# Weight splits, residual loads and table loads re-placed around the sixteen steps of an FFT convolution, with three store buffers

## The chip, the cores and the metric

The kernel runs on one core of a Trainium2 chip. The metric is device time in microseconds (us) of one execution. The kernel before was run three times: 688.23, 689.53 and 689.91 us, median 689.53.

A core has a matrix engine (TensorE, in the profile PE, its weight loads PEld), three engines for elementwise work (VectorE, DVE; ScalarE, ACT; GpSimd, POOL) and a sync engine (SyncE, SP), which here does nothing but issue transfers. An engine runs its own instructions in order. A transfer (DMA) is issued by an engine, onto that engine's queue, and carried out by the core's 16 DMA engines, which all queues share.

## The reference

One block with conditioned layer norms. A long convolution comes first (part A), a gated mixing network behind it (part B). Cut to what matters, with `L = 2048`, `D = 512` and `F = 1376`:

```python
h = layernorm(x) * (1 + ca) + sa                  # x is u; sa..gb = silu(c) @ w_mod
# part A: state-space convolution along L
K = einsum("dn,dnl,dn->dl", C, exp(dt * A * l), dt * B).real
y = irfft(rfft(pad(h)) * rfft(pad(K)))[:, :L] + h * Dskip
x = x + ga * y
h = layernorm(x) * (1 + cb) + sb
# part B: token mixing by shifts, then channel mixing
g = gelu(layernorm(h) @ w1)
x1 = h + concat(g[+1], g[-1], g[+2], g[-2]) @ w2   # each quarter of g shifted along L
x = x + gb * (x1 + gelu(layernorm(x1) @ w3) @ w4)
```

## The kernel before

**Stages.** From 0 to about 207 us the kernel generates the convolution kernel K, normalises the input, transforms it and stores that spectrum to a scratch tensor `VU` in DRAM. Then comes the second half of the convolution, which is the place of the change, up to about 316 us. The rest, to the end, is part B: products with `w1`, `w2`, `w3`, `w4`, bound by PE.

**The convolution as small transforms.** A transform of length 4096 is cut into small matrix products with tables of cosines and sines. `k_first` (line 619) is the first transform of K, eight rounds of 16 matmuls with the table `FK`; ACT and DVE copy the results out of PSUM into `VK`. Then follow sixteen *steps* `(jh, kc)`, for two halves of the channels (`jh`) and eight groups of four frequencies (`kc`). A step n consists of

- `spectrum_k` (line 664): the second transform of K, 32 matmuls with the table `T2` into two PSUM tiles `pk`. A part of them needs the negative of a piece of `T2`; that negative is a tile `T3`, which `flip` (line 658) makes on POOL, two instructions for two steps.
- `multiply` (line 685): on DVE, four products of `pk` with the input's spectrum `us` (line 690, tiles `ma` and `mb`) and two sums (line 692, tiles `zc`).
- `back` (line 695): eight short matmuls with the table `Gm` into `pz`, for the step before (n - 1); ACT copies them to a tile `z`, and POOL issues two transfers that store `z` to the scratch tensor `ZT[jh]` in DRAM (line 706). `z` comes from the pool `s2` with two buffers, so that ACT may write a new `z` only when the store of the one before the last has landed.
- `spectrum_u` (line 642) for step n + 1: PE reads a block `ld` of `VU`, and ACT copies the results to `us`.

DVE, ACT and POOL run this in the order in which it is written here (`manual_schedule`).

**The transfers.** Blocks `ld` (0.524 MB each) come from a pool `ldp` with seven buffers. A block holds a part of `VU` for `spectrum_u` (`load_vu`, line 640, issued three steps ahead), or a part of `ZT` for the inverse transform (`load_inv`, line 721), or two quarters of `w1`. SP issues all of these, the four pieces of the residual x (`load_x`, 1.05 MB each, into the tile `X2`, which the profile calls `KX` after the buffer it reuses), the table `FI` of the inverse transform (1.05 MB, during step 9) and `w2`.

**The inverse** of a half `jh` needs all eight `kc` of `ZT[jh]`. It is cut into four groups g of two halves each (`inv_half`, line 726): 16 half-size matmuls from four blocks, and DVE adds the result to `X2` (line 734). `inverse(0, 0)` stands in step 12, `inverse(0, 3)` in step 13, `inverse_parts(0, 1)` in step 15. For `ZT(0)` the four blocks of the first groups are asked for in step 10, and the other four in step 13.

**Behind the steps.** The last store of `ZT(1)` is issued by SP and ACT in two parts, and its reads follow at once (lines 1167 ff.). Until they land, PE has little to do: `inv_half(0, 2, ...)` from `ZT(0)`, and `keep(6)` (line 1180, its matmuls line 1165), six matmuls on a quarter of `w1h` whose result nobody uses. In the profile the first inverse matmuls from `ZT(1)` write the PSUM tile `py`. The text calls this stretch the hole.

**Split weights.** Each weight matrix is used as a sum of two parts. ACT makes the high part, `w1h` or `w2h` (line 115, the helper `act`), and DVE the rest, `w1l` or `w2l`, by a subtraction (line 756). `w1` and `w2` have four such pairs each. The splits of `w1` stand in steps 9 and 10 and work from blocks `ld`; those of `w2` stand in steps 14 and 15 and work in place, out of `w2l`. `w2`, `w3` and `w4` were copied earlier from the inputs to scratch tensors `Dw` in DRAM by POOL's queue, beside the generation of K; `w1` is read from the input.

Of the kernel before, what the change touches and what calls it, by code (L numbers as in the profile page):

```python
# [106 lines left out]
def body(ctx, tc, A):  # L107
# [12 lines left out]
    WD = {k: dpool.tile(list(A[k].shape), F32, name="D" + k) for k in ("w2", "w3", "w4")}  # L120
# [390 lines left out]
    for k in range(2):  # L511
        side[28 + 3 * k].append(lambda i=k * 256: P.dma_start(WD["w2"][i:i + 256], A["w2"][i:i + 256]))
# [94 lines left out]
    Gm = c2.tile([128, 2, 64], F32, name="Gm")  # L607
# [3 lines left out]
    ldp = a2.enter_context(pool("ldp", bufs=7))  # L611
# [44 lines left out]
    t3s = {}  # L656

    def flip(kc):
        t = t3s[kc] = c2.tile([128, 8, 64], F32, name="T3", bufs=3)
        for gh in range(2):  # L660
            r = slice(gh * 64, gh * 64 + 64)
            P.tensor_scalar(t[r], T2[kc // 4][r, kc % 4 * 4:kc % 4 * 4 + 8, 64 - gh * 64:128 - gh * 64], -1.0, None, op0=OP.mult)

    def spectrum_k(jh, kc):
        p = [kbank([128, 2, 2, 128]) for gh in range(2)]
        for i in range(2):
            for ro in range(2):
                for ri in range(2):
                    for kk in range(2):
                        for gh in range(2):  # L670
                            k1 = kc * 4 + 2 * kk + i
                            rows = slice(gh * 64, gh * 64 + 64)
                            w = T2[k1 // 16][rows, k1 % 16]
                            if ri == gh:
                                w = w[:, ro * 64:ro * 64 + 64]
                            elif ro == ri:
                                w = w[:, gh * 64:gh * 64 + 64]
                            else:
                                w = t3s[kc // 2 * 2][rows, k1 % 8]
                            T.matmul(p[gh][kk * 64:kk * 64 + 64, i, ro], w,  # L680
                                     VK[jh][rows, ri * 32 + k1].rearrange("p j g -> p (j g)"),
                                     start=(ri == 0), stop=(ri == 1), skip_group_check=True)
# [12 lines left out]
    def back(jh, kc):  # L695
        zc = zcs.pop((jh, kc))
        z = s2.tile([128, 4, 256], F32, name="z")
# [25 lines left out]
    def load_x(g):  # L723
        Y.dma_start(X2[:, g * 4:g * 4 + 4].rearrange("p b d -> p (b d)"), A["x"][g])
# [18 lines left out]
    def weights(pl, src, rows, cols, name, ntile):  # L743
# [3 lines left out]
        def load(stage, i, m=1, c0=0, c1=cols):  # L747
            n = min(128, rows - i * 128)
            w = stage(m, c1 - c0) if stage else lo.bitcast(F32)[:, i:i + m, c0:c1]
            Y.dma_start(w[:n], src[i * 128:i * 128 + (m - 1) * 128 + n, c0:c1].rearrange("(a p) n -> p a n", p=n))  # L750
# [8 lines left out]

    def two(m, n):  # L760
        return block().rearrange("p (a c) b -> p a (c b)", a=2)
# [335 lines left out]
    with tc.manual_schedule():  # L1097
        load_vu(*steps[0])
        flip(0)
        Y.dma_start(Gm, A["G"].rearrange("p (a b) -> p a b", a=2))  # L1100
        for r in range(8):
            k_first(r)
            if r == 3:
                load_vu(*steps[1])
            if r == 6:
                load_vu(*steps[2])
        us = spectrum_u(*steps[0])
        split = None
        for n, st in enumerate(steps):
            p = spectrum_k(*st)  # L1110
            multiply(*st, us, p)
            if n == 7:
# [4 lines left out]
                W1h, W1l, ldw1 = weights(pw1, A["w1"], 512, 512, "w1", 4)  # L1117
# [6 lines left out]
            if n + 3 < 16:  # L1124
                load_vu(*steps[n + 3])
            if n % 2 == 0 and n < 14:
                flip(steps[n + 2][1])
            if n in (3, 4, 6, 8):
                load_x(n - 3 if n < 5 else n // 2 - 1)
            if n == 9:  # L1130
                Y.dma_start(FI, A["FI"].rearrange("p (a b c) -> p a b c", a=32, b=2))
            if split:
                split()
                split = None
            if n in (8, 9):
                split = ldw1(two, n % 2 * 2, 2)
# [12 lines left out]
            if n in (14, 15):  # L1149
                w2s.pop()()  # L1150
# [24 lines left out]
        for b in (14, 15, 4, 5, 6, 7):  # L1175
            half_stat(b, 0)
        for k in (1, 2):
# [124 lines left out]
```

## Time and profile before

| | |
|---|---|
| median of three runs | 689.53 us |
| the profiled execution, its own time | 691.26 us |
| its span | 689.5 us |
| PE busy (weight loads) | 642.6 us (509.2) |
| DVE busy | 498.0 us |
| ACT busy | 331.2 us |
| POOL busy | 124.8 us |
| moved by DMA | 86.42 MB, 125 GB/s on average |

The span runs from the first instruction to the last; the execution's own time holds a little more at its ends. Busy PE over the whole kernel says that part B and the generation of K are PE's. The page's 40 slices show where this is not so (each digit is a tenth of the slice, a slice is 17.2 us, and the 14th to the 19th hold 224 to 327 us):

```profile
PE   1899999999999998977998999999999999999996
DVE  7899999999996887986987967464574536363522
ACT  3878988889875557432444623123131312222121
POOL 4011112112103355413741101001010000000000
DMA  8603264643739997967387010020100201010001
GB/s 299 284 2 79 75 218 105 209 121 85 275 85 317 354 335 258 346 204 226 108 257 240 1 32 32 16 77 15 47 31 17 77 1 62 1 49 13 1 31 31
```

From the 13th to the 19th the row DMA stands between 6 and 9, and the row GB/s between 204 and 354; behind the 22nd both are low. How to read a row of the chain of waits, in what follows: the time at which a piece of work in the chain began, its length, the engine or DMA, and the tile. A row of the waits names who waited and for whom: total us, count, the longest.

### The profile page before, as it was taken

The numbers are of one execution on the slowest core, as the hardware profiler recorded it, in microseconds if no ns is written. First come the engines' busy times: TensorE is split into PE (matmuls) and PEld (weight loads), VectorE is DVE, ScalarE is ACT, GpSimd is POOL, SyncE is SP. The second block draws the span as 40 slices with busy tenths as digits, with TensorE's granted clock in tenths as the row PEclk, the third lists the DMA queues.
The fourth block names the chain that finished last, engine by engine and source line by source line (L and its number), as shares of the span: only waits on it lengthen the run. The fifth ranks groups of instructions, "written<-read, shape, count | busy, mean of one in ns | idle before, by whom it ended". The sixth has DMA issues, their size and how long they took to land.

```text
span 689.5 us, 16884 instructions
## 1 busy us (share of the span) xinstructions
PE 642.6 (93%) x7195; PEld 509.2 (74%) x7195; DVE 498.0 (72%) x795; ACT 331.2 (48%) x505; POOL 124.8 (18%) x236
## 2 busy tenths in 40 slices
PE   1899999999999998977998999999999999999996
PEld 0456655655569776634887889999899889898895
DVE  7899999999996887986987967464574536363522
ACT  3878988889875557432444623123131312222121
POOL 4011112112103355413741101001010000000000
PEclk9999999999999999998999999999999999999999
DMA  8603264643739997967387010020100201010001
GB/s 299 284 2 79 75 218 105 209 121 85 275 85 317 354 335 258 346 204 226 108 257 240 1 32 32 16 77 15 47 31 17 77 1 62 1 49 13 1 31 31
DMA packets 51091, 86.42 MB, mean 125 GB/s; under 512 B 4676, under 2 KB 39496, under 8 KB 48424
## 3 DMA queue, kind: packets, MB, share of 16 engines
q1 hardware_dynamic: 46712, 66.74, 30.1%
q0 software_dynamic: 3440, 17.57, 7.4%
q8 instruction: 56, 0.92, 0.6%
q10 hardware_dynamic: 864, 1.05, 0.5%
q14 instruction: 19, 0.16, 0.1%
HBM read 59.12 MB, written 32.90 MB: 133 GB/s over the span
## 4 chain that ended last, share of the span: by engine, by line
PE 70%; DVE 6%; DMA 5%; ACT 3%; POOL 2%; issue 1%; ACTq 0%; SPq 0%; DVEq 0%; POOLq 0%
PE pm L841 7%; PE pm L838 7%; PE pm L839 7%; PE xx L448 7%; PE pa L954 6%; PE pa L955 6%; PE pa L962 6%; PE kp L498 3%; DMA ZT<-z 3%; PE ph L893 2%; PE ph L895 2%; PE ph L892 2%; DMA ld<-ZT 2%; PE pu L426 2%; PE pT L803 2%; PE pk L626 2%
## 5 line engine op out<-in xcount | busy, mean ns | idle before, releaser
L115 ACT ACTIVATE gh<-pm 128x512 fp32r<-128x512 f32 (+1 forms) x48 | 26.9, 560 | 200.7 <-PE pm L841 200.7
L838 PE MATMUL pm<-nh,w3h 128*128 128x256 f32 (+1 forms) x352 | 86.6, 281 | 2.7 <-ACT nh L115 2.7
L839 PE MATMUL pm<-nh,w3l 128*128 128x256 f32 (+1 forms) x352 | 86.3, 280 | 0.1
L946 DVE TENSOR_TENSOR gl<-gf,gh 128x512 fp32r<-128x512 f32 (+1 forms) x48 | 30.8, 643 | 68.4 <-ACT gf L115 68.4
L954 PE MATMUL pa<-w4h,gh 128*128 128x512 f32 (+1 forms) x176 | 69.6, 395 | 0.0
L838 PEld LDWEIGHTS pm<-nh,w3h 128*128 128x128 f32 (+1 forms) x352 | 66.0, 187 | 4.4 <-ACT nh L115 2.9
L955 PE MATMUL pa<-w4l,gh 128*128 128x512 f32 (+1 forms) x176 | 68.9, 392 | 0.0
L839 PEld LDWEIGHTS pm<-nh,w3l 128*128 128x128 f32 (+1 forms) x352 | 65.9, 187 | 2.2 <-DVE w3l L756 0.5
L765 POOL TENSOR_TENSOR rs<-mv,eps_t 128x1 f32<-128x1 f32 (+1 forms) x39 | 11.0, 282 | 282.4 <-DVE mv L771 265.4
L841 PE MATMUL pm<-nl,w3h 128*128 128x256 f32 (+1 forms) x352 | 55.0, 278 | 0.0
L449 PE MATMUL xx<-MG,ON 64*128 64x512 f32 x160 | 48.1, 397 | 0.0
L962 PE MATMUL pa<-w4h,gl 128*128 128x512 f32 (+1 forms) x176 | 48.0, 390 | 0.0
L448 PE MATMUL xx<-MG,ON 64*128 64x512 f32 x160 | 48.0, 396 | 0.0
L841 PEld LDWEIGHTS pm<-nl,w3h 128*128 128x128 f32 (+1 forms) x352 | 47.0, 187 | 0.0
L898 DVE TENSOR_TENSOR h<-h,ph 128x512 f32<-128x512 f32 x16 | 11.0, 687 | 45.1 <-PE ph L895 45.1
L466 DVE SCALAR_TENSOR_TENSOR e<-tr,p 128x512 f32<-128x512 f32 x64 | 41.1, 684 | 1.5 <-ACT tr L115 1.5
L498 PEld LDWEIGHTS kp<-e,e 128*32 128x32 f32 x2048 | 30.1, 110 | 12.7 <-issue 7.6
L475 DVE TENSOR_TENSOR e<-tr,p 128x1024 f32<-128x1024 f32 x32 | 39.0, 1220 | 0.0
L476 DVE TENSOR_TENSOR e<-tr,m 128x1024 f32<-128x1024 f32 x32 | 39.0, 1219 | 0.0
L115 ACT ACTIVATE p<-xx 128x1024 f32<-128x1024 f32 (+1 forms) x40 | 37.5, 979 | 2.2 <-PE xx L252 1.0
L962 PEld LDWEIGHTS pa<-w4h,gl 128*128 128x128 f32 (+1 forms) x176 | 33.0, 188 | 7.3 <-DVE gl L946 0.2
L115 ACT ACTIVATE tr<-xx 128x1024 f32<-128x1024 f32 x32 | 33.0, 1030 | 9.6 <-PE xx L449 7.9
(236 smaller groups left out, 1731.6 us busy)
## 6 DMA issues: line engine op xcount, KB each, us to landing
VU<-vs SPq DMA_DIRECT2D x64, 128.0 KB, 3.7
ld<-VU SPq DMA_DIRECT2D x16, 512.0 KB, 7.4
ZT<-z POOLq DMA_DIRECT2D x30, 256.0 KB, 6.2
ld<-ZT SPq DMA_DIRECT2D x12, 512.0 KB
Dw<-in_w POOLq DMA_DIRECT2D x8, 688.0 KB, 4.7
xu<-in_u SPq DMA_DIRECT2D x4, 1024.0 KB, 8.0
KX<-in_x SPq DMA_DIRECT2D x4, 1024.0 KB, 8.0
GD<-go SPq DMA_DIRECT2D x16, 256.0 KB, 2.3
```

The costliest lines, as they stand in the source:

```text
L115: return S.activation(out, in_, f, bias=bias, scale=scale)
L448: T.matmul(x[:, :512], la, ma, start=(i == 0), stop=(i == len(ops) - 1))
L449: T.matmul(x[:, 512:], lb, mb, start=(i == 0), stop=(i == len(ops) - 1))
L466: V.scalar_tensor_tensor(e0[:, 1, a], tr[:, 1, 0], 1.0 - 2.0 * a, mg[:, a], op0=OP.mult, op1=OP.mult)
L475: V.tensor_mul(e0[:, 0], tr[:, 0, 0:1].to_broadcast([128, 2, 512]), mg)
L498: T.matmul(kp[32 * j:32 * j + 32, (k % 2) * 4 + g], e1[:, r, d], e0[:, r, :, d * 32:d * 32 + 32], start=(r == 0), stop=(r == 1), skip_grou ...
L838: T.matmul(p, wh[:, k, c], hi[k], start=(k == 0), stop=False)
L839: T.matmul(p, wl[:, k, c], hi[k], start=False, stop=False)
L841: T.matmul(p, wh[:, k, c], lo[k], start=False, stop=(k == 3))
L954: T.matmul(acc[i], gh[:m, e, s], W4h[:m, f], start=(f == 0), stop=False)
L955: T.matmul(acc[i], gh[:m, e, s], W4l[:m, f], start=False, stop=False)
L962: T.matmul(acc[i], gl[:m, e, s], W4h[:m, f], start=False, stop=(f == 10))
```

## The change

- **z and the flips.** `z` gets three buffers. `flip` makes all negatives in eight instructions ahead of step 0, into one tile `T3`, rather than sixteen along the steps.
- **Queues.** The pieces of x, both halves of `w1` and both of `w2` are loaded by POOL's queue rather than SP's: x in steps 2, 4, 6 and 8, `w1` in steps 9 and 11, `w2` in steps 12 and 13. They stand between POOL's stores of `z`.
- **Blocks.** `ldp` has six buffers rather than seven. `w1` needs no block any more: it is loaded into `w1l` and split in place, as `w2` was. `w1` is copied to scratch ahead of time too, 1.05 MB more beside the generation of K.
- **VU** is asked for four steps ahead up to step 12, with three blocks in the first transform.
- **Tables.** `FI` is loaded in the seventh round of `k_first`. `Gm` takes the buffer of `FK`, so that its load must wait for the last matmul of `k_first`; it is written behind it.
- **Splits.** All eight pairs of `w1` and `w2` stand in the hole: on ACT behind its DMA issues, on DVE behind the statistics that follow `inv_half(0, 2, ...)`. `keep(6)` reads the first `w1h`, and so stands behind the first of these.

The diff, cut to its core:

```diff
-    WD = {... for k in ("w2", "w3", "w4")}
+    WD = {... for k in ("w1", "w2", "w3", "w4")}
...
     for k in range(2):
-        side[28 + 3 * k].append(lambda i=k * 256: P.dma_start(WD["w2"][i:i + 256], A["w2"][i:i + 256]))
+        for j, w in enumerate(("w1", "w2")):
+            side[24 + 4 * j + 2 * k].append(lambda w=w, i=k * 256: P.dma_start(WD[w][i:i + 256], A[w][i:i + 256]))
...
-    Gm = c2.tile([128, 2, 64], F32, name="Gm")
...
-    ldp = a2.enter_context(pool("ldp", bufs=7))
+    ldp = a2.enter_context(pool("ldp", bufs=6))
...
+    T3 = s2.tile([128, 32, 64], F32, name="T3", bufs=1)
-    def flip(kc):
-        t = t3s[kc] = c2.tile([128, 8, 64], F32, name="T3", bufs=3)
...
+    def flip(i):
+        for a in range(0, 16, 8):
...
-        z = s2.tile([128, 4, 256], F32, name="z")
+        z = s2.tile([128, 4, 256], F32, name="z", bufs=3)
...
     def load_x(g):
-        Y.dma_start(X2[:, g * 4:g * 4 + 4]...
+        P.dma_start(X2[:, g * 4:g * 4 + 4]...
...
         load_vu(*steps[0])
         flip(0)
-        Y.dma_start(Gm, A["G"]...)
+        flip(1)
         for r in range(8):
             k_first(r)
-            if r == 3:
-                load_vu(*steps[1])
+            if r in (1, 3, 5):
+                load_vu(*steps[r // 2 + 1])
             if r == 6:
-                load_vu(*steps[2])
+                Y.dma_start(FI, A["FI"]...)
+        Gm = pa12.tile([128, 2, 64], F32, name="FK")
+        Y.dma_start(Gm, A["G"]...)
...
-            if n + 3 < 16:
-                load_vu(*steps[n + 3])
-            if n % 2 == 0 and n < 14:
-                flip(steps[n + 2][1])
-            if n in (3, 4, 6, 8):
-                load_x(n - 3 if n < 5 else n // 2 - 1)
-            if n == 9:
-                Y.dma_start(FI, A["FI"]...)
-            if split:
-                split()
-                split = None
-            if n in (8, 9):
-                split = ldw1(two, n % 2 * 2, 2)
+            if n < 13 and n != 10:
+                load_vu(*steps[n + 4 - n // 10])
+            if n in (2, 4, 6, 8):
+                load_x((0, 3, 1, 2)[n // 2 - 1])
+            if n in (9, 11):
+                wsplits.append(ldw1(None, n // 10 * 2, 2, q=P))
+            if n in (12, 13):
+                wsplits.append(ldw2(None, n % 2 * 2, 2, q=P))
...
                 inverse(0, 0)
-                w2s = [ldw2(None, 2 * i, 2) for i in range(2)]
...
-            if n in (14, 15):
-                w2s.pop()()
...
         for b in (14, 15, 4, 5, 6, 7):
             half_stat(b, 0)
+        for f in wsplits:
+            f()
         for k in (1, 2):
             load_inv(1, k)
```

How this stands on the engines: the rows below are the instructions of one engine in its order; a row is the line of the code, the operation, the tile written and the tile or tensor read, the size, and how many alike follow each other.

POOL through the steps, before (`T` from `xu` is a flip, `T2` being kept in the buffer of `xu`; `ZT_61` and `ZT_62` are the two halves of ZT):

```order
L662 TENSOR_SCALAR T_3081<-xu 64x512 x2
L662 TENSOR_SCALAR T_3355<-xu 64x512 x2
L706 DMA ZT_61<-z 32x2x1024 x4
L662 TENSOR_SCALAR T_3500<-xu 64x512 x2
L706 DMA ZT_61<-z 32x2x1024 x4
L662 TENSOR_SCALAR T_3646<-xu 64x512 x2
L706 DMA ZT_61<-z 32x2x1024 x4
L662 TENSOR_SCALAR T_3792<-xu 64x512 x2
L706 DMA ZT_61<-z 32x2x1024 x4
```

and the same engine in the changed kernel, from `T3` to the step 13 (`KX<-in_x` is a piece of x, `Dw_64` and `Dw_65` are the copies of `w1` and `w2`):

```order
L662 TENSOR_SCALAR T_3079<-xu 64x512 x8
L706 DMA ZT_61<-z 32x2x1024 x4
L724 DMA KX<-in_x 128x2048
L706 DMA ZT_61<-z 32x2x1024 x4
...
L706 DMA ZT_62<-z 32x2x1024 x2
L750 DMA w1l<-Dw_64 128x2x512
L706 DMA ZT_62<-z 32x2x1024 x4
L750 DMA w1l<-Dw_64 128x2x512
L706 DMA ZT_62<-z 32x2x1024 x2
L750 DMA w2l<-Dw_65 128x2x512
L706 DMA ZT_62<-z 32x2x1024 x2
L750 DMA w2l<-Dw_65 128x2x512
L706 DMA ZT_62<-z 32x2x1024 x4
```

Each load of x or of a weight now stands between two stores of z, and the flips stand ahead of all of them.

SP from the first block of VU to the reads of ZT(0), before (`Dw_64` is the copy of `w2` here, since `w1` has none):

```order
L640 DMA ld<-VU 128x4x256
L1100 DMA Gm<-in_G 128x128
L640 DMA ld<-VU 128x4x256 x6
...
L750 DMA ld<-in_w 128x2x512
L640 DMA ld<-VU 128x4x256
L721 DMA ld<-ZT_61 128x4x256 x4
L640 DMA ld<-VU 128x4x256 x2
L750 DMA w2l<-Dw_64 128x2x512 x2
L721 DMA ld<-ZT_61 128x4x256 x4
```

and in the changed kernel (`FK<-in_G` is the load of Gm into the buffer of FK):

```order
L640 DMA ld<-VU 128x4x256 x4
L1103 DMA FI<-in_FI 128x2048
L1105 DMA FK<-in_G 128x128
L640 DMA ld<-VU 128x4x256 x10
L721 DMA ld<-ZT_61 128x4x256 x4
L640 DMA ld<-VU 128x4x256 x2
L721 DMA ld<-ZT_61 128x4x256 x4
```

SP's queue now holds the blocks and the two tables alone.

DVE from the last step into the hole, before:

```order
L756 TENSOR_TENSOR w2l<-w2l,w2h 128x512 x2
L690 TENSOR_TENSOR ma<-pk_4460,us 128x512
...
L756 TENSOR_TENSOR w2l<-w2l,w2h 128x512 x2
L734 TENSOR_TENSOR KX<-pk_4515,KX 128x2x256
L734 TENSOR_TENSOR KX<-pk_4524,KX 128x2x256
L734 TENSOR_TENSOR KX<-py,KX 128x2x256 x2
L784 BN_STATS st_80<-KX 128x6 x6
L734 TENSOR_TENSOR KX<-py,KX 128x2x256
```

and now:

```order
L734 TENSOR_TENSOR KX<-pk_4489,KX 128x2x256
L734 TENSOR_TENSOR KX<-pk_4498,KX 128x2x256
L734 TENSOR_TENSOR KX<-py,KX 128x2x256 x2
L781 BN_STATS st_81<-KX 128x6 x6
L756 TENSOR_TENSOR w1l<-w1l,w1h 128x512 x4
L756 TENSOR_TENSOR w2l<-w2l,w2h 128x512 x4
L734 TENSOR_TENSOR KX<-py,KX 128x2x256
```

The subtractions of the splits stand between the statistics of the last `ZT(0)` group and the first addition from `ZT(1)`, the one with `py` in the last row.

More of the change, by code (lines that the diff above doesn't have):

```diff
@@ L678, in spectrum_k @@
                             else:
-                                w = t3s[kc // 2 * 2][rows, k1 % 8]
+                                w = T3[rows, k1]
                             T.matmul(p[gh][kk * 64:kk * 64 + 64, i, ro], w,
@@ L758, in weights @@
         return hi, lo, load
-    def two(m, n):
-        return block().rearrange("p (a c) b -> p a (c b)", a=2)
     def rstd(r, v):
```

23 lines of the change are left out of this document (11 added, 12 removed).

## The prediction

> **What bounds the kernel now.** I read the chain of waits first, then windows, then who waits for whom, then the engines' timelines from 207 us (the first DFT of the kernel spectrum) to 325 us. Before and after that stretch the changed kernel runs the same instructions on PE, ACT and DVE.
>
> The chain of work that ended last, two places of it (start us, us, what):
>
> ```profile
> 234.17 8.87 DMA ZT<-z
> 243.84 1.57 PE pz L702 x8
> ...
> 289.33 1.99 PE pz L731 x32
> 291.66 7.89 DMA ld<-ZT
> 299.59 1.93 PE pk L731 x32
> 301.59 1.64 PE pz L702 x8
> 305.03 2.69 DMA ZT<-z
> 308.51 4.98 DMA ld<-ZT
> 313.63 2.42 PE py L731 x17
> 316.07 0.70 DVE KX L734
> ```
>
> Three kinds of DMA stand in it: a store of z that a later step waits for, the second batch of reads of ZT(0) (from 291.66), and the round trip of ZT(1) behind the last step (305.03 to 313.5; from here "the hole"). The sum below is kept on one point, the start of `back` of step 15 (301.59), and on what the hole takes behind it.
>
> The windows (us, PE, PEld, DVE, ACT, POOL busy, PE clock, DMA share, GB/s):
>
> ```profile
> 224.00:244.00 20.00, 18.15 (x433) 15.16 (x432) 15.56 (x26) 9.83 (x20) 5.32 (x6) 1.00 1.01 358
> ...
> 280.00:290.00 10.00, 8.98 (x168) 5.49 (x168) 10.00 (x20) 4.50 (x10) 4.56 (x6) 1.00 1.03 363
> ```
>
> The DMA engines are full in these windows and move about 0.36 MB per us; no engine's own work explains the steps alone. The waits between 224 and 316 us:
>
> ```profile
> ACT z L115 <- DMA ZT<-z: 8.7, 3, 4.3
> ...
> DVE ma L690 <- ACT us L115: 5.9, 2, 3.2
> ...
> PE pk L680 <- POOL T L662: 1.6, 3, 0.5
> ```
>
> ACT stands for a z buffer whose store has not landed; `us`, next on ACT's queue, is late; DVE, which paces the steps, loses 5.9 us to that in two places. DVE's timeline, the first product of steps 0, 3, 8 and 12:
>
> ```profile
> 227.31 0.69 DVE L690 TENSOR_TENSOR ma<-pk,us 128x512 f32<-128x512 f32 x1 [2.12 <-PE pk L680]
> ...
> 238.42 0.69 DVE L690 TENSOR_TENSOR ma<-pk,us 128x512 f32<-128x512 f32 x1
> ...
> 263.19 0.69 DVE L690 TENSOR_TENSOR ma<-pk,us 128x512 f32<-128x512 f32 x1 [2.69 <-ACT us L115]
> ...
> 281.76 0.68 DVE L690 TENSOR_TENSOR ma<-pk,us 128x512 f32<-128x512 f32 x1
> ```
>
> Steps 0 to 3 run unhindered: (238.42 - 227.31) / 3 = 3.70 us each. Twelve such steps would bring step 12 to 227.31 + 44.4 = 271.7; it starts at 281.76. The 10.1 us are the 5.9 above, the splits of w1 with ACT's wait ahead of them (about 4), and small waits.
>
> **The change, part by part.** *Steps 0 to 11.* The third z buffer takes the 5.9 us away: a store may then take three steps, 11.1 us, against 8.87 for the longest in the chain. The splits leave the steps:
>
> ```profile
> L756 DVE TENSOR_TENSOR w1l<-ld,w1h 128x512 fp32r<-128x512 f32 x4 | 3.0, 788 | 1.0 <-ACT w1h L115 1.0
> ...
> L756 DVE TENSOR_TENSOR w2l<-w2l,w2h 128x512 fp32r<-128x512 f32 x4 | 2.6, 690 | 0.3 <-ACT w2h L115 0.3
> ```
>
> So DVE could be at step 12 by 271.7. What is late next is the DMA: not a byte leaves this stretch (FI, x, w1, w2, VU and ZT are all still moved in it). In step 12 `inverse(0, 0)` needs four reads of ZT(0), 0.524 MB each, issued once the store of step 7 has landed:
>
> ```profile
> 265.06 1.07 POOL L706 DMA_DIRECT2D ZT<-z  x2 [1.46 <-ACT z L115]
> ```
> ```profile
> 269.70 4.17 SPq L721 DMA_DIRECT2D ld<-ZT  x4
> ```
>
> That store was issued 1.9 us behind the start of step 8 and landed 4.6 later. With step 8 at 227.31 + 29.6 = 256.9 the reads go out at 263.4; the x block that now stands ahead in POOL's queue may cost a little, so I take 264.5. What they share the engines with: on POOL's queue two or three stores, a rest of the last x block, one or two halves of w1, between 1.6 and 3.1 MB. The reads are 2.1 MB, and issue and landing cost about 3 us more. PE asks for them at 271.7 + 2.0 = 273.7 (before, the inverse came at 283.77, 2.0 behind its step). Lower end: SP's queue is served alone, 264.5 + 3 + 2.1 / 0.36 = 273.3, so PE does not wait. Upper end: all of POOL's 3.1 MB first, 264.5 + 3 + 5.2 / 0.36 = 281.9. The nearest row is the store of 8.87 us: the engines moved 8.87 x 0.358 = 3.2 MB meanwhile, and only 0.52 to 1.05 MB of that can be POOL's, so that queue got a sixth to a third, SP's the rest. At a quarter the reads take 2.1 / 0.27 = 7.8, 275.3; the fourth waits for its block until about 267, so I take 277, 6.8 before 283.77.
>
> The Trainium skill (DMA: Bandwidth & Descriptors, Queues, rings and completion order) has it that each DMA engine takes turns between its queues, packet by packet. The share of a sixth to a third of that store speaks for turns of unequal size; the even split is a rival below.
>
> *Steps 12 to 15.* From the start of the first inverse to the end of `inverse(0, 3)` nothing changes, 283.77 to 291.32, 7.5 us: after, 284.5. The second batch of reads waits for it. Before, three of its four reads waited and landed 8.2 us later (299.55). After, with six blocks, the buffer of the fourth is also one that this inverse reads: one read more, 0.524 / 0.36 = 1.45. The second half of w2, now issued on POOL's queue in step 13, costs 0 to 1.45; I take 1.45, as these engines are full. So 11.1: 295.6. `inverse_parts(0, 1)` takes 2.0 as before, and `back` of step 15 starts at 297.6: **4.0 earlier**. The 2.6 us of the w2 splits buy nothing of their own, since DVE is early for this read either way. Ends: 273.7 + 7.5 + 9.65 + 2.0 = 292.9 (8.7 earlier) and 281.9 + 7.5 + 12.5 + 2.0 = 303.9 (2.3 later; 12.5 if two more POOL transfers come first).
>
> *The hole.* ACT and DVE now run eight splits each there. ACT is free of its DMA issues at 308.89:
>
> ```profile
> 307.94 0.95 ACTq L721 DMA_DIRECT2D ld<-ZT  x2
> ```
> ```profile
> 270.78 1.18 ACT L115 ACTIVATE w1h<-ld 128x512 fp32r<-128x512 f32 x2
> ```
>
> Four pairs of 1.18 end at 313.6 and DVE's last subtraction at 314.3, ahead of 316.07: the round trip of ZT(1) hides them. Without that cover they would cost 5.6. A gain comes with them. `keep(6)`, six matmuls on w1h, ran before the wait and must now wait for the first split:
>
> ```profile
> 305.51 1.67 PE L1165 MATMUL pT<-w1h 128*128 128x512 f32 x6
> ```
> ```profile
> 311.00:313.00 2.00, 0.00 (x0) 0.00 (x0) 0.00 (x0) 0.00 (x0) 0.00 (x0) 0.86 0.97 306
> 313.00:315.00 2.00, 1.37 (x13) 0.73 (x17) 0.00 (x0) 0.00 (x0) 0.00 (x0) 0.50 1.07 362
> ```
>
> PE is idle from 307.2 to 313.6, the granted clock falls to 0.50 from 312 on, and the first inverse costs 2.42. After, PE is idle from 305.5 to 309.5 (308.89 plus one ACT of 0.6) and from 311.2 to 313.6, both gaps shorter than the 5 us that it took here. At full clock 17 such matmuls take half, so **1.2 earlier**; ends 0 and 1.4. By the Trainium skill (TensorE: Matmul & The Clock Gate, Part 1: The HAM clock gate) a free-running window of about 3.4 us without work is enough; a 4.0 us gap could hold one, and then this term is nothing and the time 685.5.
>
> *At no cost.* The new Gm waits for the last matmul of the first DFT (224.4), with all later SP loads queued behind it:
>
> ```profile
> 213.09 1.61 SPq L1100 DMA_DIRECT2D Gm<-in_G  x1
> ```
> ```profile
> DMA to landing us min/median/max: 2.4/3.6/8.1
> ```
>
> With that issue and the landing of the VU stores (128 KB, second row) it is there at 228.4 to 229.6, up to 234.1; its first reader runs at 230.45. So nothing, at worst 3.7 early in the steps, where step 12 still waits for reads. The flips on POOL, all eight ahead of step 0:
>
> ```profile
> 209.31 6.20 POOL L662 TENSOR_SCALAR T<-xu 64x512 f32<-64x512 f32 x4 [26.16 <-DMA wm<-in_TU]
> ```
>
> Eight take 12.4 us. Even from 212.8 they end at 225.2, and only the first pair is wanted by then. The copy of w1 adds 1.05 MB near 171 to 185 us; the engines have room soon after (2 GB/s, share 0.00):
>
> ```profile
> 195.00:200.00 5.00, 5.00 (x95) 3.13 (x96) 5.00 (x8) 3.04 (x4) 0.00 (x0) 1.00 0.00 2
> ```
>
> Hence nothing, at most 1.05 / 0.36 = 2.9. In the hole two reads instead of one wait for the last py, up to 1.45 us, with 5 us until their matmuls: nothing.
>
> **The sum.** The profiled execution is 691.26 (span 689.5), 1.73 above the median of 689.53. Less 4.0 and 1.2 it is 686.1, so the median comes to **684.3**.
>
> **The rivals.** *The transfers keep up* (SP's queue served first): `back` of step 15 at 292.9, with 1.4 in the hole: 689.53 - 8.7 - 1.4 = 679.4. For it: 5.9 us of the old stalls were stores waiting on a slower queue. Against: the engines are full. Chance 0.15. *Even split*: 2.1 MB at half of 0.36 need 11.7, reads there at 264.5 + 3 + 11.7 = 279.2, inverse done at 286.7, batch of 12.5 (both queues full throughout) and 2.0: 301.2, 0.4 earlier; with the hole 687.9. The change would do its part in the steps and bring nothing. Chance 0.18. *Slower*: what moved to POOL's queue goes first. Its rows are 4 to 8 KB against 1 KB of the ZT reads. The second batch then takes the place of the z stall: 2.3 later, clock gain lost, 691.8. It decides once inverse plus batch exceed what steps 0 to 11 gained, that is, if the first reads land after 279.6 with a batch of 12.5. Against: the store of 8.87 us. Chance 0.09.
>
> **How the numbers follow.** Forecast 0.58, the others 0.15, 0.18, 0.09. Some 2.1 us (0.3%) is what a measurement can tell from no change. Faster: 0.15, nearly all of 0.58, a little of the even split: 0.74; same 0.17; slower 0.09. The range, 679.5 to 690.0, takes in the ends of the reads short of the slower rival.
>
> **What would show it.** Right: no ACT wait on ZT<-z, steps 0 to 11 at 3.7 us, step 12 near 272 with PE then waiting for ld<-ZT until about 277, a second such wait of 11 us behind `inverse(0, 3)`, `back` of step 15 near 297.6, a granted clock near 1.0 at the first py. Wrong: z stalls that stay, a wait at Gm, or splits that end after the first py.

## The result and the profile after

| | before | changed |
|---|---|---|
| median of the runs (us) | 689.54 (688.23 to 689.91) | 700.81 (700.34 to 702.30) |
| profiled execution, its own time (span) | 691.26 (689.5) | 700.34 (698.6) |

The ratio is 1.0171, 95% interval 1.0150 to 1.0191: the changed kernel is 11.3 us slower, where 5.2 less was forecast. The two profiled executions differ by 9.1 us; the traces below can explain these 9.1 and not the rest. The chain of work of the changed kernel, the same places as before (start us, us, what):

```profile
268.59 17.17 DMA ld<-ZT
...
285.90 3.62 PE pz L731 x32
...
293.15 1.86 PE pz L731 x32
...
296.17 6.80 DMA ld<-ZT
302.97 10.43 issue
...
315.18 2.68 DMA ZT<-z
...
323.53 1.97 PE py L731 x16
```

The store of z is gone from the steps. In its place stands one read of ZT(0) of 17.17 us, the last of its batch, and the second batch behind it ends later than before: `py` starts at 323.53, 9.9 us behind the 313.63 of the kernel before. The row `issue` of 10.43 us means that the chain found no releaser for that stretch; PE's timeline further down shows what fills it, the end of a wait for `ld<-ZT` and the inverse behind it. DVE's timeline shows that the steps did their part:

```profile
226.05 0.69 DVE L690 TENSOR_TENSOR ma<-pk,us 128x512 f32<-128x512 f32 x1 [2.11 <-PE pk L680]
...
237.16 0.69 DVE L690 TENSOR_TENSOR ma<-pk,us 128x512 f32<-128x512 f32 x1
...
273.97 0.68 DVE L690 TENSOR_TENSOR ma<-pk,us 128x512 f32<-128x512 f32 x1
...
287.90 0.69 DVE L734 TENSOR_TENSOR KX<-pz,KX 128x512 f32<-128x512 f32 x1 [10.25 <-PE pz L731]
```

Steps 0, 3 and 12 start at 226.05, 237.16 and 273.97: (237.16 - 226.05) / 3 = 3.70 us each, and step 12 is 7.8 us ahead of before. Then DVE, and PE ahead of it, wait for the reads. The transfers between the issue and the landing of those reads, 266 to 286 us, by queue (packets, MB, share of the 16 engines' time; q0 is POOL's queue, q1 SP's) and by issue (count, KB, median us to landing; for the four reads the profile has the landing of the last alone):

```profile
DMA packets 4084, 6.99 MB, mean 349 GB/s; under 512 B 275, under 2 KB 3144, under 8 KB 4040
q0 software_dynamic: 1129, 4.01, 53.4%
q1 hardware_dynamic: 2952, 2.94, 45.9%
ld<-ZT SPq DMA_DIRECT2D x4, 512.0 KB, 17.2
w1l<-Dw POOLq DMA_DIRECT2D x2, 512.0 KB, 7.9
```

The engines are full, and of 6.99 MB only 2.1 are the reads that PE waits for. POOL's weights land in 7.9 us, the last read takes 17.2. The windows of the changed kernel over that wait, behind it, and in the hole (us, busy of PE, PEld, DVE, ACT, POOL, clock of PE, DMA share, GB/s):

```profile
276.00:286.00 10.00, 0.14 (x6) 0.13 (x8) 1.65 (x3) 1.76 (x4) 1.82 (x3) 0.66 1.05 385
286.00:293.00 7.00, 7.00 (x120) 4.02 (x119) 4.11 (x9) 0.67 (x2) 0.00 (x0) 0.76 0.10 32
315.00:320.00 5.00, 0.20 (x5) 0.08 (x1) 2.79 (x9) 0.76 (x2) 0.00 (x0) 1.00 0.54 137
320.00:326.00 6.00, 5.20 (x30) 2.97 (x34) 5.29 (x9) 3.50 (x7) 0.00 (x0) 0.51 1.07 353
```

PE idles 10 us and its granted clock falls (0.66 on average there); as soon as PE works again, the DMA engines idle (share 0.10 from 286 to 293), since the second batch of reads waits in the program behind `inverse(0, 3)`. Before, the same stretch had:

```profile
286.00:293.00 7.00, 7.00 (x184) 5.01 (x180) 6.74 (x14) 2.56 (x5) 3.68 (x4) 1.00 0.91 330
```

PE's timeline of the changed kernel gives the cost of the low clock, from here on called cold (a granted clock near 0.50; warm is 1.00):

```profile
285.90 3.62 PE L731 MATMUL pz<-ld,FI 128*32 128x256 f32 x32 [9.86 <-DMA ld<-ZT]
...
293.08 1.93 PE L731 MATMUL pz<-ld,FI 128*32 128x256 f32 x32
...
307.69 3.64 PE L731 MATMUL pk<-ld,FI 128*32 128x256 f32 x32 [5.85 <-DMA ld<-ZT]
311.26 1.99 PE L702 MATMUL pz<-zc,FK 64*64 64x512 f32 x8
```

The same 32 matmuls take 3.62 and 3.64 us behind the two waits and 1.93 otherwise. `back` of step 15 starts at 311.26, against 301.59 before. These are 9.7 us; the spans differ by 9.1, so the loss lies ahead of this point, and 0.6 are won back behind it.

### The profile page after: what moved, and what is told of

It reads as the page before. It is cut to its first block, busy times and chain, and to the rows that moved or that the text cites. A ratio compares the mean times of both kernels' runs of the same rounds, so it can differ in the third digit from the quotient of the medians.

```text
span 698.6 us, 16871 instructions
## 1 busy us (share of the span) xinstructions
PE 641.0 (92%) x7195; PEld 509.0 (73%) x7195; DVE 497.4 (71%) x795; ACT 331.4 (47%) x505; POOL 118.3 (17%) x238
## 3 DMA queue, kind: packets, MB, share of 16 engines
q10 hardware_dynamic: 864, 1.05, 0.5%
## 4 chain that ended last, share of the span: by engine, by line
PE 73%; DVE 13%; DMA 5%; ACT 3%; issue 3%; POOL 1%; SPq 0%; ACTq 0%; DVEq 0%; POOLq 0%
PE pm L838 8%; PE pm L835 8%; PE pm L836 7%; PE xx L448 7%; PE pa L951 6%; PE pa L952 6%; PE pa L959 6%; DMA ld<-ZT 4%; PE pk L680 3%; PE kp L498 3%; PE ph L890 2%; PE ph L892 2%; PE ph L889 2%; PE pu L426 2%; PE xx L252 2%
## 5 line engine op out<-in xcount | busy, mean ns | idle before, releaser
L448 PE MATMUL xx<-MG,ON 64*128 64x512 f32 x160 | 47.1, 390 | 0.0
L449 PE MATMUL xx<-MG,ON 64*128 64x512 f32 x160 | 47.1, 390 | 0.0
L115 ACT ACTIVATE z<-pz 128x512 f32<-128x512 f32 x32 | 17.4, 595 | 47.4 <-PE pz L702 37.0
L498 PEld LDWEIGHTS kp<-e,e 128*32 128x32 f32 x2048 | 30.1, 110 | 12.7 <-issue 7.9
## 6 DMA issues: line engine op xcount, KB each, us to landing
ld<-VU SPq DMA_DIRECT2D x16, 512.0 KB, 11.1
```

Of the source, the lines that this page charges most:

```text
L115: return S.activation(out, in_, f, bias=bias, scale=scale)
L448: T.matmul(x[:, :512], la, ma, start=(i == 0), stop=(i == len(ops) - 1))
L449: T.matmul(x[:, 512:], lb, mb, start=(i == 0), stop=(i == len(ops) - 1))
L498: T.matmul(kp[32 * j:32 * j + 32, (k % 2) * 4 + g], e1[:, r, d], e0[:, r, :, d * 32:d * 32 + 32], start=(r == 0), stop=(r == 1), skip_grou ...
```

## The experiments

Three theories went into them. **A**: what POOL's queue is given beside and behind the reads of ZT(0) takes the engines from them. **B**: x is asked for too late, since POOL issues it behind its stores. **C**: six blocks, and the second batch that waits for them, cost the time. The cold clock was tested by itself. Edits are to the changed kernel unless a line says otherwise; times are medians, beside about 689 for the kernel before on the same chips.

**Smaller rows on POOL's queue** (`small_packets`).

```diff
-        P.dma_start(X2[:, g * 4:g * 4 + 4]..., A["x"][g])
+        for c in range(0, 512, 256):
+            P.dma_start(X2[:, g * 4:g * 4 + 4, c:c + 256], A["x"][g]...[:, :, c:c + 256])
```

The loads of `w1` and `w2` on POOL's queue are cut in the same way.

> The changed kernel with every load of x, w1 and w2 on POOL's queue cut into two transfers with rows of 1 KB rather than 4 to 8 KB; same bytes, same queue, same places. In the changed kernel PE waits for the first four reads of ZT(0) until 285.9 us. Theory A (the DMA engines take turns by packets, so POOL's packets of 4 to 8 KB take three to four times the bytes of SP's reads of 1 KB): SP's queue gets about half of the bytes between 250 and 286 us rather than a quarter to a half, the first inverse starts near 280 and the time falls by 5 to 7, to 694 to 696. Theory B (x is issued some 17 us later than before, because POOL issues it behind its stores, and the room that the DMA engines had before 236 us is lost): nothing changes by more than 1 us, 700 to 701. Theory C (six blocks hold the reads back): 700 to 701.

701.67 us: no change. But the edit didn't do what it was for. POOL's queue from 250 to 264 us in the changed kernel, and then in this one:

```profile
q0 software_dynamic: 867, 3.81, 73.0%
```
```profile
q0 software_dynamic: 1157, 4.00, 78.2%
```

The queue's packets, those of the stores among them, went from 4.4 KB on average only to 3.5 KB: rows of 1 KB that go to one partition did not travel as packets of 1 KB. Whether the size of packets sets the share of a queue stays open.

**x earlier** (`x_early`): `for g in {0: (0, 3), 2: (1,), 4: (2,)}.get(n, ()): load_x(g)`.

> The changed kernel with x asked for earlier on POOL's queue: two pieces in step 0, one in step 2, one in step 4, rather than one each in steps 2, 4, 6 and 8. Theory B (late x): between 224 and 236 us the engines move about 370 rather than 230 to 290 GB/s, which is 1.4 MB or 3.8 us, so the first inverse starts near 282 rather than 285.9, and the time is about 697. Theory A (turns by packets): two pieces of 8 KB rows ahead of the first stores take the turns from the reads of VU and the stores, steps 1 to 4 slow down, and what is won later is lost there: 699 to 702. Theory C (six blocks): no change, 700 to 701.

700.23 us. The windows of the changed kernel and then of this one:

```profile
224.00:236.00 12.00, 11.52 (x300) 9.96 (x297) 9.72 (x17) 7.21 (x15) 1.32 (x3) 1.00 0.82 258
```
```profile
224.00:236.00 12.00, 11.52 (x302) 9.94 (x296) 9.77 (x17) 7.26 (x15) 1.32 (x4) 1.00 1.04 356
260.00:268.00 8.00, 8.00 (x196) 6.93 (x190) 7.77 (x14) 5.50 (x12) 2.89 (x5) 1.00 0.51 119
```

The early room was filled as theory B says, and the engines were half idle when the reads were issued; the inverse still started at 285.1. So moving bytes ahead of the reads brought nothing while the same weights and stores came beside and behind them. B falls.

**The weights away from the reads**: later on POOL's queue (`w_late`, the first edit) and in their places on SP's (`w_on_sp`, the second).

```diff
-            if n in (9, 11):
-                wsplits.append(ldw1(None, n // 10 * 2, 2, q=P))
-            if n in (12, 13):
-                wsplits.append(ldw2(None, n % 2 * 2, 2, q=P))
+            if n == 15:
+                for i in (0, 2):
+                    wsplits.append(ldw1(None, i, 2, q=P))
+                for i in (0, 2):
+                    wsplits.append(ldw2(None, i, 2, q=P))
```
```diff
             if n in (9, 11):
-                wsplits.append(ldw1(None, n // 10 * 2, 2, q=P))
+                wsplits.append(ldw1(None, n // 10 * 2, 2, q=Y))
             if n in (12, 13):
-                wsplits.append(ldw2(None, n % 2 * 2, 2, q=P))
+                wsplits.append(ldw2(None, n % 2 * 2, 2, q=Y))
```

> The changed kernel with all four loads of w1 and w2 on POOL's queue in step 15 rather than in steps 9, 11, 12 and 13. Theories A and B alike: 1.57 MB that POOL's queue moved ahead of the first reads of ZT(0) are gone, at 0.37 MB per us 4.2 us, and 0.52 MB are gone from the second batch, 1.4 us: the first inverse starts near 281.7 and the time is 695 to 696. Theory C (six blocks hold the reads back): the first inverse stays near 286 and only the 1.4 us of the second batch go, 699 to 700. If the splits in the hole then wait for the weights, up to 3 us of it come back.

> The changed kernel with the four loads of w1 and w2 on SP's queue instead of POOL's, in the same steps. In the changed kernel 1.57 MB of them share the engines with the first reads of ZT(0), which land at 285.8. Theory A (what POOL's queue is given behind the reads is served beside them): on SP's queue only the first half of w1 stands ahead of the reads and the rest behind them; 1.05 MB at 0.36 MB per us are 2.9 us, so the first inverse starts near 283 and the time is 697 to 698. Theory A2 (the reads land when all that was asked for up to then has moved, whatever the queue): the inverse stays at 285 to 286, 700 to 701.

694.37 us (ratio to before 1.0076, 1.0051 to 1.0101) and 694.29 us (1.0064, 1.0040 to 1.0089), 6.4 and 6.5 less than the changed kernel. PE's first inverse in the one and the other:

```profile
280.53 3.49 PE L731 MATMUL pz<-ld,FI 128*32 128x256 f32 x32 [4.23 <-DMA ld<-ZT]
```
```profile
281.99 3.64 PE L731 MATMUL pz<-ld,FI 128*32 128x256 f32 x32 [4.71 <-DMA ld<-ZT]
```

Theory A holds for the first reads: 5.4 and 3.9 us earlier. The same bytes on SP's queue, most of them behind the reads, do little harm there. `w_late` gained about 1 us more than was expected, `w_on_sp` about 3.

**All loads on SP's queue** (`x_w_on_sp`: `Y` for `P` in `load_x` too).

> The changed kernel with x and w1, w2 on SP's queue again, in the places of the changed kernel; z, T3, blocks and splits stay. Theory A: at most the first half of w1 stands ahead of the first reads, POOL's queue has stores alone, and the first inverse starts near 281 as with the weights alone on SP, or 1 to 3 us earlier if x matters too: 690 to 694. Theory C: the second batch still goes out behind inverse(0, 3), so that no more than this is won, and the time stays above 689.5.

693.01 us, ratio 1.0039 (1.0011 to 1.0067): x adds nothing that can be told from `w_on_sp`.

**Weights early** (`w_early`: x as in `x_early`, `w1` in step 8 and `w2` in step 9).

> The changed kernel with x asked for in steps 0, 0, 2 and 4 and all of w1 and w2 in steps 8 and 9, all on POOL's queue. Asking for x early alone left the engines about half idle from 260 to 268 us (0.11 to 0.14 MB per us) and gained nothing, since POOL's 3.6 MB behind the reads stayed. Theory A: the weights now fill that hole, the reads share the engines with stores alone and the first inverse starts at 278 to 280, rather than 285.9; the second batch of reads loses 0.52 MB beside it: the time is 691 to 693. Theory C (six blocks hold the reads back): the first inverse may come earlier, but the reads of the second batch still go out only behind inverse(0, 3), with idle DMA engines ahead of them, so that the time stays at or above 689.5 in any case; 692 to 695.

697.44 us, with runs from 694.1 to 702.2. `w1` went out at 260.5 and `w2`, behind the next store on POOL, only at 264.7, just as the reads did on SP at 264.6; the inverse started at 282.5, not at 278 to 280. The time is above what either theory gave.

**The inverses together** (`pair`).

```diff
                 inverse(0, 0)
+                inverse(0, 3)
...
-            if n == 13:
-                inverse(0, 3)
                 for k in (1, 2, 5, 6):
                     load_inv(0, k)
```

> The changed kernel with inverse(0, 3) straight behind inverse(0, 0) in step 12, and the second batch of reads issued there. Theory C (six blocks): the four blocks come free one step earlier, the DMA engines, idle from 288 to 293 us in the changed kernel, start on the second batch 4 us sooner, and inverse(0, 1), which waited for it until 307.7, starts near 303: 696 to 697. If the second batch is bound by the bytes on POOL's queue instead: 699 to 701.

693.10 us, ratio 1.0050 (1.0028 to 1.0071): 7.7 less than the changed kernel, more than expected. Its windows:

```profile
286.00:292.00 6.00, 6.00 (x78) 3.26 (x81) 2.26 (x4) 0.00 (x0) 0.00 (x0) 0.65 0.08 25
292.00:300.00 8.00, 8.00 (x209) 6.52 (x205) 8.00 (x16) 3.99 (x8) 1.86 (x4) 1.00 0.92 302
```

The issues of the second batch in the changed kernel, and then in this one:

```profile
293.23 4.04 SPq L721 DMA_DIRECT2D ld<-ZT  x4
```
```profile
291.68 2.01 SPq L721 DMA_DIRECT2D ld<-ZT  x4
```

The first inverse is where it was (285.89), and the engines still idle from 286 to 292. But the four reads are all out by 293.7 rather than 297.3, and one step more now stands behind them, so that PE has work while they land and no longer waits: `inverse(0, 1)` ran at 302.43 with a warm clock, against 307.69 cold, and ended 7.0 us earlier (304.4, 311.3).

**Seven blocks.** `z3_7blocks` makes room for the seventh by making the flips along the steps again; `z2_7blocks` gives up the third z buffer for it; `z3_6blocks` is the kernel before with three z buffers and six blocks.

```diff
-    ldp = a2.enter_context(pool("ldp", bufs=6))
+    ldp = a2.enter_context(pool("ldp", bufs=7))
...
-    T3 = s2.tile([128, 32, 64], F32, name="T3", bufs=1)
...
+        t = t3s[kc] = s2.tile([128, 8, 64], F32, name="T3", bufs=2)
```

> The changed kernel with seven blocks; the memory for it comes from making the flips along the steps again, two T3 tiles at a time. If the six blocks cost the second batch (theory C): one read of it goes out ahead of inverse(0, 3) and lands beside step 13, inverse(0, 1) starts 1.5 to 4 us earlier, 697 to 699. If the queue alone does it (theory A): 700 to 701, as in the changed kernel.

> The changed kernel with two z buffers and seven blocks, as before the change. Theory A (the first reads wait for what POOL's queue is given beside them, and the steps, 8 us early in the changed kernel, buy nothing): the stalls of ACT on the stores come back and step 12 starts later, near 280, but the first inverse starts within 2 us of 285.9; the seventh block lets one read of the second batch out before inverse(0, 3), 1.5 us less behind it: 697 to 701. Rival Z (the third z buffer is a gain that the rest spoils): the stalls of 5.9 us come on top, 704 to 707.

> The kernel before with three z buffers and, since the memory holds no more, six blocks rather than seven; x, w1, w2, FI and the splits stay where they were before. Theories A and B: what made the changed kernel slow was the queue on which x and the weights are loaded, and this kernel leaves them on SP's: the two stalls of 5.9 us go, the reads of ZT(0) set the end of the steps as forecast, and the time is 685 to 688, against 689.5 before. Theory C (six blocks hold the reads back): slower than before, 691 to 697.

698.85 us for `z3_7blocks`: 2.0 less than the changed kernel, though its interval (1.0114 to 1.0158) just overlaps the other's. `z2_7blocks` gave 687.76, 694.35, 700.18 and 700.71 us, median 697.26, too far apart for a verdict. But the fastest of these executions was profiled. In it the reads went out at 263.4, and the first inverse followed its step without a wait, with the weights on POOL's queue as in the changed kernel:

```profile
278.44 1.93 PE L731 MATMUL pz<-ld,FI 128*32 128x256 f32 x32
```

So that placement alone does not delay the reads in every execution; what made the others of this kernel slower stays open.

`z3_6blocks` is slower than the kernel before, 692.50 us, ratio 1.0040 (1.0019 to 1.0062): without any stall of ACT on the stores. It started its first inverse at 281.24, 2.5 us earlier than before, but cold, and issued the second batch from 288.4, against 283.9 before:

```profile
281.24 3.44 PE L731 MATMUL pz<-ld,FI 128*32 128x256 f32 x32 [2.74 <-issue]
```

That is the range of theory C, not of theory A: some 3 us are lost with a third buffer and six blocks although no weights are on POOL's queue. A seventh block is worth some 2 us in the changed kernel, if that; by itself it is not the cause.

**The clock** (`warm`, and `warm9` with 9 and 4 in place of 20 and 8).

```diff
+    def warm(n):
+        d = psa.tile([128, 2, 256], F32, name="pz").rearrange("p a b -> p (a b)")
+        for _ in range(n):
+            T.matmul(d, ident, T2[1][:, 0:4].rearrange("p a b -> p (a b)"), start=True, stop=True)
...
             if n == 15:
+                warm(8)
                 i1 = inverse_parts(0, 1, psb, "pk2")
...
             if n == 12:
+                warm(20)
                 inverse(0, 0)
```

> The changed kernel with matmuls whose result nobody uses, 20 ahead of inverse(0, 0) and 8 ahead of inverse_parts(0, 1), in the time in which PE waits for reads. In the changed kernel PE idles for 9.9 and 5.9 us there, the granted clock falls to 0.50, and the two inverses take 3.6 us each instead of 1.9, the back behind the second 2.0 instead of 1.6. If the clock is what costs this: 3.7 us less, 697. If these pieces are bound by something else, or the clock stays down: 700 to 701.

> The kernel warm with fewer unused matmuls: 9 ahead of inverse(0, 0), 4 ahead of inverse_parts(0, 1). In warm 20 of them ran from 276 to 292.9, 0.84 us each, past the landing of the reads at 283.2, but the granted clock stayed at 1.0 and the inverse took 1.9 instead of 3.6. Now they end near 283.6 and 306.4. If the cold clock is a part of the loss: 1.7 for each of the two inverses and 0.4 for the back go, 697 against 700.8. If not: 700 to 701.

`warm` took 705.48 us, a miss: its 20 matmuls ran for 17.4 us, longer than the wait. `warm9` took 698.32 us, 2.5 less than the changed kernel, but its four runs spread from 695.3 to 701.5, and the intervals of the two kernels overlap. PE's timeline in its profiled execution, the slowest of the four:

```profile
275.61 7.99 PE L742 MATMUL pz<-xu,ident 128*128 128x512 f32 x18
...
285.53 1.93 PE L731 MATMUL pz<-ld,FI 128*32 128x256 f32 x32 [1.92 <-DMA ld<-ZT]
...
291.02 1.93 PE L731 MATMUL pz<-ld,FI 128*32 128x256 f32 x32
...
307.76 3.64 PE L731 MATMUL pk<-ld,FI 128*32 128x256 f32 x32 [3.60 <-DMA ld<-ZT]
```

After 1.92 us of idling the inverse is warm, after 3.60 us it is cold. So the cold clock costs 1.7 us at an inverse. In this execution the gain does not last: `inverse(0, 3)` starts 2.1 us earlier than in the changed kernel (291.02, 293.08), but `inverse(0, 1)`, behind the second batch, at 307.76 as there (307.69). How much of the whole loss is the clock's is not shown.

**Combinations.** `x_early_w_late_pair` and the same with six unused matmuls in the hole (`x_early_w_late_pair_fill`); `w_sp_pair` (`w_on_sp` and `pair`); `z3_7blocks_sp_pair`, which takes `z3_7blocks`, x on SP's queue, `w1` there in steps 8 and 9 ahead of the reads, `w2` there behind the second batch, and `pair`; and as controls `before_pair`, the same move of the inverse in the kernel before, and `w_sp_pair_z2`, `w_sp_pair` with two z buffers.

> Three edits of the changed kernel together: x asked for in steps 0, 0, 2 and 4, w1 and w2 all in step 15, and inverse(0, 3) with the second batch of reads straight behind inverse(0, 0) in step 12; all else as in the changed kernel (three z buffers, six blocks, splits in the hole). Theory A (the first reads wait for what POOL's queue is given beside and behind them): with x done by 253 us and no weights, the reads issued near 265.7 share 4.2 MB with four stores alone and land near 278; PE hardly idles; the second batch goes out by 282 and lands near 292, back of step 15 starts near 296 (311.3 in the changed kernel, 301.6 before), and the time is 684 to 687, below the kernel before. Rival R (the reads on SP's queue take 13 us or more whatever stands beside them): the first inverse starts at 280 or later at a cold clock, and the time is 689 to 692.

> The kernel x_early_w_late_pair with six matmuls of ident with FI, whose result nobody uses, behind inv_half(0, 2, ...) in the hole. In the changed kernel PE idles there from 315.1 to 319.9, the granted clock falls to 0.50 from 320.1, and the first inverse of ZT(1) takes 3.6 rather than 1.9. If the clock is what this costs: 1 to 2 us below x_early_w_late_pair. If the matmuls of this stretch are not on the path: no difference.

> The changed kernel with the weights on SP's queue (alone: 694.3) and inverse(0, 3) with the second batch in step 12 (alone: 693.1). If the two remove different waits, 6.5 and 7.7 us add up in part: the first inverse near 282, the second batch out by 287 and landed by 297, 688 to 690. If they remove the same bytes from the same place, as the three edits together suggest: 692 to 694.

> Both causes taken away: three z buffers and seven blocks (flips along the steps, two T3 tiles), x in steps 2 to 8 and w1 in steps 8 and 9 on SP's queue ahead of the first reads, w2 on SP's queue behind the second batch, both inverses and the second batch in step 12, splits in the hole. If queue and blocks are the cause: no stalls of z, step 12 near 272, the reads in near 277, the second batch out by 282 and in by 291, back of step 15 near 296 against 301.6 before, and 683 to 686, faster than both kernels. If something else holds the reads: 689 or more.

> The kernel before with inverse(0, 3) and the second batch of reads straight behind inverse(0, 0) in step 12. If putting the inverses together is the whole of what made w_sp_pair and z3_7blocks_sp_pair faster than the kernel before: 686 to 688. If the kernel before has no idle DMA engines there to use (they are full from 272 to 300 us but for 0.2 of 288 to 292) and the gain is that of the steps: 689 to 690, the same as before.

> w_sp_pair (687.7) with two z buffers instead of three. If the third buffer buys nothing, because the reads and not the steps set the first inverse: 687 to 688.5, with stalls of ACT on the stores of z in the steps. If it is part of the gain: 690 or more.

| kernel | median (us) | ratio to before, 95% |
|---|---|---|
| x_early_w_late_pair | 693.04 | 1.0062 (1.0039 to 1.0085) |
| x_early_w_late_pair_fill | 693.81 | 1.0072 (1.0058 to 1.0086) |
| w_sp_pair | 687.71 | 0.9977 (0.9958 to 0.9996) |
| z3_7blocks_sp_pair | 687.13 | 0.9962 (0.9945 to 0.9979) |
| before_pair | 690.46 | 1.0022 (1.0009 to 1.0035) |
| w_sp_pair_z2 | 688.20 | 0.9986 (0.9966 to 1.0006) |

The first of them won its time up to `back` of step 15 (at 300.3, against 311.26) and lost 4.5 us of it in the hole. Its chain and then that of `z3_7blocks_sp_pair`:

```profile
303.30 7.97 DMA ZT<-z
317.11 1.97 PE py L731 x16
```
```profile
268.50 11.49 DMA ld<-ZT
280.12 3.81 PE pz L731 x64
...
296.75 1.60 PE pz L702 x8
300.15 2.65 DMA ZT<-z
...
308.31 2.19 PE py L731 x17
```

With 2.1 MB of weights just issued on POOL's queue, the last store of z takes 7.97 us instead of 2.7. That fits theory A once more, at another wait. The unused matmuls in the hole kept the clock up, 1.93 instead of 3.56 us for the first 32 matmuls with `py`, and brought no gain that these runs can tell.

In `z3_7blocks_sp_pair` the reads land at 280, the two inverses run warm in 3.81 us, `back` of step 15 starts at 296.75 and `py` at 308.31, 5.3 us ahead of the kernel before; the profiled execution, 686.11 us, is one of its faster ones. It is faster than both kernels, by 0.4% than the one before; 683 to 686 was expected, 687.1 came. `w_sp_pair` lies below both too, within 0.6 us of it, with two edits. `before_pair` gains nothing: 0.2% slower, so putting the inverses together is not by itself what makes `w_sp_pair` fast. The third z buffer is worth 0.5 us in `w_sp_pair`, which the intervals don't tell from nothing.

## Why the prediction was wrong

Point by point, by the terms of its sum:

- **Steps 0 to 11** were right in the mechanism: no wait of ACT on a store, 3.70 us for the first three steps, step 12 at 273.97 where 271.7 was forecast. But step 0 was 1.3 us early, and the twelve steps took 47.9 us, not 44.4: DVE waited for `pk` of PE six times, 4.2 us in all, and what held PE the trace does not show.
- **The first reads** are the step that failed: in at 277, it said; they were in at 285.8. Of 8.8 us, 1.7 come from the issue (266.2, not 264.5). The rest is the sharing: with the weights gone from beside the reads they were in 5.4 us earlier (`w_late`), and 3.9 earlier with the same bytes on SP's queue (`w_on_sp`). The sum counted 1.6 to 3.1 MB on POOL's queue beside the reads and a quarter of the engines for it; the trace has 4.01 MB, 57% of all bytes moved there, and 53.4% of the engines' time. The upper end of the range, all of POOL's 3.1 MB first, gave 281.9 and was passed, because too few bytes stood in it: four stores of 0.52 MB, three halves of weights and a rest of x make the 4.0, and on SP's own queue 2.94 - 2.10 = 0.8 MB more went to the two last blocks of VU, issued behind the reads and moved beside them.
- **The quarter** came from a store of 8.87 us, taken as a sign that SP's queue gets the larger share. By queue, the kernel before had in those 9 us (234 to 243):

```profile
q1 hardware_dynamic: 1145, 2.05, 70.8%
q0 software_dynamic: 298, 1.00, 27.7%
```

  The share was read rightly, if low (1.00 of 3.09 MB is about a third, the upper end of the reading), but at a time when POOL's queue had nothing but two steps' stores and SP's two blocks of VU and a piece of x, and it was carried over to a time when the large transfers stood on POOL's. The rule on turns in the Trainium skill (DMA: Bandwidth & Descriptors, Queues, rings and completion order), which the prediction set aside for this row, is nearer to the changed kernel's 53.4 to 45.9% of the engines' time, though in recorded packets the turns are 1129 to 2952. The even split was given as a rival at 687.9; its share came true, its bytes did not.
- **From the first inverse to the end of `inverse(0, 3)`**: 7.5 forecast, 295.01 - 285.90 = 9.1 measured. **The second batch**: 11.1 forecast, 307.69 - 295.01 = 12.7. **`inverse_parts(0, 1)`**: 2.0 forecast, 311.26 - 307.69 = 3.6. Two of these three errors, 1.6 each, go with the cold clock, which the sum had in the hole and not behind the waits for the reads; `warm9` shows it for the first, 7.4 us from 285.53 on with a warm clock. The 1.6 of the batch are not taken apart. With the 8.9 by which the first inverse was late, the three make the 13.7 between 297.6 and 311.26.
- **The place of the second batch** was left as it is, behind `inverse(0, 3)`. So its reads go out late, and PE has too little to do until it needs them; `pair` shows that this was worth 7.7.
- **The hole**: the splits are hidden, as forecast, but the 1.2 us did not come. From `back` of step 15 to the first addition from `py`, 14.48 us before (316.07 - 301.59) and 14.26 after (325.52 - 311.26). PE idles from 315.1 to 319.9, 4.8 us rather than 4.0, and the clock falls to 0.51 in the next window. The prediction held gaps under 5 us to be harmless; 2.74 us in `z3_6blocks`, 3.60 in `warm9` and 4.23 in `w_late` were not. The page on the clock gate (TensorE: Matmul & The Clock Gate, Part 1: The HAM clock gate in the Trainium skill) speaks of about 3.4 us, and by it the term was nothing, as it came out here. The 2.74 us are shorter than its window; there the measurement decides.
- **The third buffer** did what was forecast in the steps, but no run shows it as a gain: with the waits behind the steps mended it makes 0.5 us, which is not told from nothing (`w_sp_pair_z2`), and by itself with six blocks it is a loss (`z3_6blocks`).
- **At no cost** were Gm, the flips, and the copy of `w1`, as forecast: step 0 starts at 226.05, 1.3 us earlier than before.

The rival that came nearest is the slower one: what moved to POOL's queue takes the place of the stall of z. Its point of decision, the first reads in after 279.6, was right; its price, 2.3 us, was a quarter of the true one.

The two causes, the weights beside the reads (6.5 us alone) and the late second batch (7.7 alone), nearly add up: `w_sp_pair` takes both away and is 13.1 us below the changed kernel. Not settled is what sets a queue's share (size of packets, their number, or time), since no run changed the packets alone, and why one execution of `z2_7blocks` had its reads in time with the weights on POOL's queue.

## What to carry to other kernels

When a stall is removed from a stretch whose DMA engines are full, list for the next wait all bytes that any queue will be given until it lands, those issued behind it too, and divide them by the measured rate; a share read from another place holds only for what the queues held there. Large transfers that nobody waits for soon did less harm here on the queue of the urgent ones, behind them; on a second queue they ran beside them. And a wait on PE can have a second price, slow matmuls behind it: here after idling for 2.74 us and more, not after 1.92.

## What was not expected of the hardware

- A read of 0.52 MB on SP's queue took 17.2 us, the other three of its batch ahead of it, while transfers of the same size on POOL's queue landed in 7.9 us.
- Cutting the rows of the loads on POOL's queue to 1 KB (for x from 8 KB) left the queue's packets at 3.5 KB on average, against 4.4.
- Clock: idle for 1.92 us, warm; idle for 2.74 us (`z3_6blocks`) or 3.60 us (`warm9`), cold, and 32 matmuls of 128x256 took 3.44 and 3.64 instead of 1.93 us.
